# Nine due times for nine decoding steps: the weight chunks of an attention and gated-FFN kernel

## The chip, the cores and the metric

One core of a Trainium2 chip runs the whole program. The metric is the device time of one execution in microseconds (us), the median of the timed runs. Engines: TensorE (PE in the rows, its weight loads PEld), VectorE (DVE), ScalarE (ACT), GpSimd (POOL), and SyncE (SP), which here only issues DMAs.

## The reference

Attention with rotary position embedding over 8 batches × 8 heads (576 positions, 64 wide), its output taken as the input of a gated feed-forward block:

```python
q_rot, k_rot = rotate(q), rotate(k)
scores = q_rot @ k_rot.T / sqrt(64); scores -= max(scores)
attn = exp(scores) / (sum(exp(scores)) + 1e-9)
x = (attn @ v) -> [8, 576, 512]
gate_pre = sum over k of conv_w[k] * x shifted by 4 - k      # causal, 5 taps
out = (sigmoid(gate_pre) * (x @ w_val)) @ w_out
```

The weights `w_val`, `w_out` (512×512) and `conv_w` are float64 (their scale factors make them so), the rest float32. The chip has no float64, so the kernel takes the weights as pairs of 32-bit words and decodes them into two float32r parts, high and low.

## The kernel before

Two heads make a pair; 32 pairs, four to a batch. For each pair the scores come in five groups (`s0` to `s4`, `s_mm`, L253) into PSUM; VectorE takes the row maxima (`max0` to `max8`, `s_max`, L259), ScalarE the exponentials (`exp0` to `exp8`, L272). Then P is transposed. In pairs 0 to 4 (keys with the ending `e`) and in the last one this is done by TensorE (`t0` to `t7`, `th`, `tm`, `thm`, L301 to L343) with copies out of PSUM by ScalarE or VectorE (`c0` to `c7`, `ch`, `cm`, `chm`, L188 and L190); in the others VectorE transposes blocks (`turn`, L287) and DMAs move them (`move`, L292). The P·V matmuls follow (`pv4`, `pv0`, `pv1`, `pvm`, L357 to L380), and two normalisations by VectorE (`norm0`, `norm1`, L406), which also free the two accumulators. The five taps (L427, L430) make the gate. After every fourth pair the feed-forward block runs in eight pieces of each of its two stages (`f0j`, `f1j`, L456).

q and k of the next pairs are rotated meanwhile: two multiplications (`mul0`, `mul1`, L210), an addition (`add`, L214), the high part (`hi`, ScalarE, L221) and the low part (`lo`, L225), on VectorE (V) or POOL (G) by the table `PICK`.

Each weight has four chunks of 128 rows. A chunk is loaded by SP (`load_weight`, L520, 512 KB), and decoded in nine steps:

- steps 0, 1, 3, 4, 5 on VectorE (L490, L492, L495, L496, L497) and step 2 on ScalarE (L493), all 128×512, in place (`weight_step`);
- step 6, `w_high`, the high part, on ScalarE (L527);
- step 7, `w_mm`, matmuls of the residue on TensorE into a PSUM bank (L532 to L534);
- step 8, `w_low`, the low part out of that bank, on ScalarE (L188).

The chunks 0 to 3 of `w_val` are called val0 to val3 below, those of `w_out` out0 to out3. Two chunks share a buffer of the kind `big`; there are three of these, and the transposed P of each pair needs one as well. PSUM has two banks of the kind `ps_t`, shared by transposes, P·V, residues and the feed-forward block.

**The order.** Every job is put down by `at(key, base, engine, ...)`; its due time is `base + DUE[key]`. `Plan.order` works it off as a list: of all jobs whose predecessors (by tokens read and written) are in the list already, the one with the smallest due time comes next; a job that needs a buffer waits aside until one is free. Each engine runs its jobs in the order of this list. So a due time is a rank, not a time, and a job never stands before one that it depends on. Jobs of VectorE and POOL which use the port that the two share are marked `port`; a POOL job is made to wait for the last marked VectorE job ahead of it in the list (`behind`), but a VectorE job does not wait by order for POOL.

All nine steps of a chunk write the chunk's token, so each follows the one before it. Before the change they share a key:

```python
for k, (e, ns) in enumerate((v, v2, ac, v2, v, v2)):
    at(f"d{n}{c}", due + 1.6 * k, e, ns, weight_step, n, c, k, ...)
at(f"d{n}{c}", due + 9.6, *ac, w_high, n, c, ...)
at(f"d{n}{c}", due + 10.4, "PE", 1950, w_mm, n, c, ...)
at(f"d{n}{c}", due + 12.5, "A", evict(x), w_low, n, c, "ENGINE", pick="dec" + n, ...)
```

with `due = 16 + 12 * c` for `w_val` and `62 + 10 * c` for `w_out`, and the load at `due - 6`.

Of the kernel before, what the change touches and what calls it, by code (L numbers as in the profile page):

```python
# [143 lines left out]
def attn_gated_ffn(ctx: ExitStack, tc: tile.TileContext, q2, k2, v2, tab, w_val, conv_w, w_out, out, collect=None):  # L144
# [4 lines left out]
    V, A, G, T, SP = nc.vector, nc.scalar, nc.gpsimd, nc.tensor, nc.sync  # L149
# [354 lines left out]
    taps = []  # L504
# [66 lines left out]
    def evict(x):  # L571
        return {"V": (x * 1.045 + 65, False), "A": (max(x * 0.83 + 50, 280), False)}
# [6 lines left out]
    def weights(n):  # L579
        x = DM  # L580
        for c in R4:
            tok = f"big/w{n}{c // 2}#{c % 2}"
            due = (16 + 12 * c) if n == "val" else (62 + 10 * c)
            at(f"l{n}{c}", due - 6, "SP", 560, load_weight, n, c, w=tok, kb=x * 1.024)
            v, v2, ac = ("V", x * 0.522 + 90), ("V", x * 1.045 + 90), ("A", x * 0.83 + 94)
            for k, (e, ns) in enumerate((v, v2, ac, v2, v, v2)):
                at(f"d{n}{c}", due + 1.6 * k, e, ns, weight_step, n, c, k, w=tok + f" w{n}{c}#lo" * (k == 5), port=e == "V")
            at(f"d{n}{c}", due + 9.6, *ac, w_high, n, c, w=f"{tok} w{n}{c}#hi")
            at(f"d{n}{c}", due + 10.4, "PE", 1950, w_mm, n, c, r=f"{tok} w{n}{c}#hi w{n}{c}#lo", w=f"ps_t/w{n}{c}", mode="f")
            at(f"d{n}{c}", due + 12.5, "A", evict(x), w_low, n, c, "ENGINE", pick="dec" + n, r=f"ps_t/w{n}{c}", w=f"w{n}{c}#lo")  # L590
# [203 lines left out]
```

## Time and profile before

| | us |
|---|---|
| timed runs, median of 3 (lowest, highest) | 659.85 (659.34, 663.73) |
| span of the profiled execution (no other time is given for it) | 660.3 |
| TensorE busy in the span | 614.9 (93%) |
| VectorE busy | 577.5 (87%) |
| ScalarE busy | 454.5 (69%) |
| POOL busy | 398.0 (60%) |

Busy time is what the profiler saw an engine execute; matmuls overlap, so a busy TensorE is not one at its peak. In the timelines a row is a start, a duration and an instruction; a bracket tells how long the engine sat idle before it, and what ended that. In the chain of waits each row is what the next one waited for.

### The profile page before, as it was taken

How to read it: one execution, taken by the hardware profiler on the slowest of the kernel's cores; microseconds unless marked ns; L12 is line 12 of the kernel's file. 1: busy time of each engine (PE TensorE's matmuls, PEld its weight loads, DVE VectorE, ACT ScalarE, POOL GpSimd, SP SyncE). 2: the span in 40 equal slices, each digit the busy share in tenths (PEclk: the TensorE clock that was granted, in tenths of full speed). 3: DMA queues.
4: the chain of work that ended last, by engine and by line, in shares of the span. 5: the costliest groups of instructions: out<-in, count | busy, mean ns of one | idle time of the engine just before them, and what ended most of it. 6: DMA issues, size and time to landing. Idle time of an engine off the chain costs nothing.

```text
span 660.3 us, 15367 instructions
## 1 busy us (share of the span) xinstructions
PE 614.9 (93%) x5720; PEld 496.2 (75%) x5720; DVE 577.5 (87%) x829; ACT 454.5 (69%) x1120; POOL 398.0 (60%) x303
## 2 busy tenths in 40 slices
PE   2889888889999999999999999999999999999897
PEld 1666665578777887888778887888788878888696
DVE  5799988898899999999999999999999999984552
ACT  3678877677667678777777677767777777763421
POOL 3333446569577877777776868687867777730210
PEclk9999999899989999999999999999999999999999
DMA  7324432259999999899999899999998989874101
GB/s 280 119 56 142 138 129 94 88 159 253 243 258 251 248 252 267 240 260 236 263 255 261 208 274 270 252 245 265 244 256 237 249 260 258 210 179 115 38 27 64
DMA packets 51481, 134.42 MB, mean 204 GB/s; under 512 B 10928, under 2 KB 20944, under 8 KB 51408
## 3 DMA queue, kind: packets, MB, share of 16 engines
q1 hardware_dynamic: 50864, 132.86, 72.5%
q8 instruction: 45, 0.74, 0.5%
q10 hardware_dynamic: 544, 0.59, 0.3%
q14 instruction: 28, 0.23, 0.1%
HBM read 62.48 MB, written 9.59 MB: 109 GB/s over the span
## 4 chain that ended last, share of the span: by engine, by line
PE 67%; DVE 17%; DMA 5%; ACT 4%; SPq 3%; issue 2%; POOL 0%; DVEq 0%; ACTq 0%
PE ps_t L456 26%; PE ps_s L253 17%; PE ps_t L367 14%; DVE nm L259 6%; DVE big L287 3%; SPq L292 3%; DMA ik<-in_k 3%; PE ps_t L357 3%; PE ps_t L328 2%; PE ps_t L301 2%; PE ps_t L372 2%; ACT p L272 2%; DVE g L430 2%; DMA big<-big 1%; DVE big L190 1%
## 5 line engine op out<-in xcount | busy, mean ns | idle before, releaser
L272 ACT ACTIVATE p<-ps_s,nm 128x576 f32<-128x576 f32 x256 | 187.8, 739 | 80.7 <-DVE nm L259 79.4
L259 DVE TENSOR_REDUCE nm<-ps_s 128x1 f32<-128x576 f32 x288 | 202.3, 744 | 23.8 <-PE ps_s L253 23.5
L253 PE MATMUL ps_s<-k,q 64*128 64x288 f32 x1536 | 143.7, 314 | 20.1 <-ACT k L221 9.1
L253 PEld LDWEIGHTS ps_s<-k,q 64*128 64x128 f32 x1536 | 111.3, 189 | 44.3 <-ACT p L272 13.5
L287 DVE STREAM_TRANSPOSE big<-p 128x1152 f32<-128x1152 f32 x104 | 139.8, 1353 | 0.0
L430 DVE SCALAR_TENSOR_TENSOR g<-x,cw,g 128x576 f32<-128x576 f32 (+1 forms) x132 | 118.2, 895 | 2.1 <-ACT g L427 0.6
L367 PE MATMUL ps_t<-big,v 128*64 128x256 f32 (+2 forms) x1024 | 118.6, 385 | 0.0
L367 PEld LDWEIGHTS ps_t<-big,v 128*64 128x64 f32 x1024 | 70.9, 138 | 46.2 <-issue 15.1
L210 POOL TENSOR_TENSOR iq<-iq,tab 128x576 f32<-128x576 f32 (+1 forms) x59 | 84.5, 1448 | 31.2 <-DMA iq<-in_q 27.8
L214 POOL TENSOR_TENSOR ik<-ik 128x576 f32<-128x576 f32 x27 | 39.0, 1443 | 75.0 <-DVE ik L210 72.8
L456 PE MATMUL ps_t<-xh,wval_hi 128*128 128x288 f32 x256 | 78.2, 305 | 2.2 <-DVE g L461 2.0
L456 PE MATMUL ps_t<-yh,wout_hi 128*128 128x288 f32 x256 | 79.0, 309 | 1.2 <-ACT yh L465 1.1
L456 PE MATMUL ps_t<-yl,wout_hi 128*128 128x288 f32 x256 | 76.5, 299 | 0.1
L225 POOL TENSOR_TENSOR k<-ik,k 128x576 fp32r<-128x576 f32 x31 | 54.6, 1761 | 36.0 <-ACT k L221 34.0
L456 PE MATMUL ps_t<-yh,wout_lo 128*128 128x288 f32 x256 | 75.9, 297 | 0.0
L456 PE MATMUL ps_t<-xh,wval_lo 128*128 128x288 f32 x256 | 75.9, 296 | 0.0
L456 PE MATMUL ps_t<-xl,wval_hi 128*128 128x288 f32 x256 | 75.3, 294 | 0.0
L469 POOL TENSOR_TENSOR yl<-g,yh 128x288 fp32r<-128x288 f32 x56 | 46.9, 845 | 32.8 <-DVE g L430 25.3
L417 POOL TENSOR_TENSOR xl<-x,xh 128x576 fp32r<-128x576 f32 (+1 forms) x33 | 48.3, 1464 | 25.9 <-ACT xh L413 16.5
L225 POOL TENSOR_TENSOR q<-iq,q 128x576 fp32r<-128x576 f32 (+1 forms) x32 | 45.5, 1423 | 15.8 <-ACT q L221 15.8
L210 POOL TENSOR_TENSOR ik<-ik,tab 128x576 f32<-128x576 f32 (+1 forms) x32 | 45.5, 1422 | 11.7 <-DVE big L492 7.4
L456 PEld LDWEIGHTS ps_t<-xh,wval_hi 128*128 128x128 f32 x256 | 48.1, 188 | 5.7 <-DVE g L461 2.3
(89 smaller groups left out, 1065.1 us busy)
## 6 DMA issues: line engine op xcount, KB each, us to landing
big<-big SPq DMA_DIRECT2D x416, 144.0 KB
ik<-in_k SPq DMA_DIRECT2D x31, 576.0 KB
iq<-in_q SPq DMA_DIRECT2D x31, 576.0 KB
v<-in_v SPq DMA_DIRECT2D x32, 320.0 KB
rb<-rd SPq DMA_DIRECT2D x64, 144.0 KB
out_t<-oo SPq DMA_DIRECT2D x64, 144.0 KB
big<-in_w_val SPq DMA_DIRECT2D x4, 512.0 KB
big<-in_w_out SPq DMA_DIRECT2D x4, 512.0 KB
```

Source lines behind the costliest of these rows:

```text
L210: eng.tensor_tensor(out=t[:, i, a:b], in0=t[:, i, a:b], in1=tabs[:, i, a:b], op=ALU.mult)
L214: eng.tensor_tensor(out=t[:, 0], in0=t[:, 0], in1=t[:, 1], op=ALU.add)
L225: eng.tensor_tensor(out=t[:, 1], in0=state[p][n + "in"][:, 0, a:b], in1=t[:, 0].bitcast(F32), op=ALU.subtract)
L253: T.matmul(out=ps[:, half, 0:288], lhsT=st["q"][rows, x, c * 128:c * 128 + 128] if c < 4 else mixq[p % 2][:, x], rhs=st["k"][rows, y, k0:k ...
L259: V.tensor_reduce(out=st[f"nm{i}"], in_=st[f"s{i}"], axis=AX.XY, op=ALU.max, negate=True)
L272: A.activation(out=pd.rearrange("p (b x) -> p b x", b=2), in_=st[f"s{i}"], func=AF.Exp, bias=st[f"nm{i}"], scale=1.0, accum_out=sums[p % 2 ...
L287: V.transpose(out=t[:, :, cs.index(c)].rearrange("p b k i -> p k b i"), in_=st[f"p{c}"].rearrange("p h s -> p (h s)").rearrange("p (k b i) ...
L367: T.matmul(out=acc[HEAD[h], 0:n], lhsT=st["v"][:, j, h, :], rhs=st["pt"][:, :, c0:c1, 5 * place(p, 2 * c0 + h) + j].rearrange("p a c i -> ...
L417: eng.tensor_tensor(out=st["xl"][:, a:b], in0=xs[p % 2][:, 4 + a:4 + b], in1=st["xh"][:, a:b].bitcast(F32), op=ALU.subtract)
L430: V.scalar_tensor_tensor(out=g, in0=x_sb[:, a + k:b + k], scalar=w, in1=g, op0=ALU.mult, op1=ALU.add)
L456: T.matmul(out=acc[:, 0:n], lhsT=wt[w][:, kc, ds], rhs=mv, start=(kc == 0 and i == 0), stop=(kc == NCH - 1 and i == 2))
L469: eng.tensor_tensor(out=ffn[b, "l", dc, lo], in0=y, in1=ffn[b, "h", dc, lo].bitcast(F32), op=ALU.subtract)
```

## The change

The key of each step gets the number of the step, and the table `DUE` a value for each of the 72 keys instead of 8. The values of the eight loads change as well. Ten other keys go from the tables (`x0`, `x2`, `x4`, `x6`, `mv0e` to `mv3e`, `ch0`, `ch0e`, which no job uses), and the entries are in another order. All other due times, all jobs and all engines are as before.

```diff
             for k, (e, ns) in enumerate((v, v2, ac, v2, v, v2)):
-                at(f"d{n}{c}", due + 1.6 * k, e, ns, weight_step, n, c, k, w=tok + f" w{n}{c}#lo" * (k == 5), port=e == "V")
-            at(f"d{n}{c}", due + 9.6, *ac, w_high, n, c, w=f"{tok} w{n}{c}#hi")
-            at(f"d{n}{c}", due + 10.4, "PE", 1950, w_mm, n, c, r=f"{tok} w{n}{c}#hi w{n}{c}#lo", w=f"ps_t/w{n}{c}", mode="f")
-            at(f"d{n}{c}", due + 12.5, "A", evict(x), w_low, n, c, "ENGINE", pick="dec" + n, r=f"ps_t/w{n}{c}", w=f"w{n}{c}#lo")
+                at(f"d{n}{c}_{k}", due + 1.6 * k, e, ns, weight_step, n, c, k, w=tok + f" w{n}{c}#lo" * (k == 5), port=e == "V")
+            at(f"d{n}{c}_6", due + 9.6, *ac, w_high, n, c, w=f"{tok} w{n}{c}#hi")
+            at(f"d{n}{c}_7", due + 10.4, "PE", 1950, w_mm, n, c, r=f"{tok} w{n}{c}#hi w{n}{c}#lo", w=f"ps_t/w{n}{c}", mode="f")
+            at(f"d{n}{c}_8", due + 12.5, "A", evict(x), w_low, n, c, "ENGINE", pick="dec" + n, r=f"ps_t/w{n}{c}", w=f"w{n}{c}#lo")
```

What the tables come to: the due time of the load, and those of the nine steps, for the values after the change as the largest so far within the chunk, since a step cannot stand before its predecessor.

| chunk | load, before → after | steps 0 to 8 before (0, 1, 2, 3, 4, 5, 6, 7, 8) | steps 0 to 8 after, largest so far |
|---|---|---|---|
| val0 | −734.8 → −2090.8 | 13.3, 14.9, 16.5, 18.1, 19.7, 21.3, 22.9, 23.7, 25.8 | −852.7, 14.9, 14.9, 20.0, 20.0, 20.0, 20.0, 20.0, 23.0 |
| val1 | −308.0 → 15.4 | 34.5, 36.1, 37.7, 39.3, 40.9, 42.5, 44.1, 44.9, 47.0 | 39.3, 39.3, 39.3, 40.8, 40.8, 40.8, 40.8, 45.2, 49.4 |
| val2 | −178.9 → −309.8 | 29.5, 31.1, 32.7, 34.3, 35.9, 37.5, 39.1, 39.9, 42.0 | 24.8, 32.1, 32.1, 34.0, 34.0, 34.0, 38.8, 40.0, 41.8 |
| val3 | −115.4 → −137.7 | 47.7, 49.3, 50.9, 52.5, 54.1, 55.7, 57.3, 58.1, 60.2 | 49.7, 49.7, 55.6, 57.4, 57.4, 57.4, 57.4, 58.6, 60.2 |
| out0 | 89.9 → 25.5 | 103.1, 104.7, 106.3, 107.9, 109.5, 111.1, 112.7, 113.5, 115.6 | 85.7, 85.7, 87.6, 111.2, 111.2, 111.2, 111.2, 116.3, 116.3 |
| out1 | 27.9 → 55.5 | 66.2, 67.8, 69.4, 71.0, 72.6, 74.2, 75.8, 76.6, 78.7 | 67.4, 71.6, 73.0, 76.1, 76.1, 76.1, 76.1, 77.8, 80.9 |
| out2 | 33.4 → 44.6 | 84.6, 86.2, 87.8, 89.4, 91.0, 92.6, 94.2, 95.0, 97.1 | 71.2, 71.2, 78.2, 90.5, 90.5, 90.5, 116.8, 123.6, 123.6 |
| out3 | 77.0 → 47.7 | 108.5, 110.1, 111.7, 113.3, 114.9, 116.5, 118.1, 118.9, 121.0 | 89.2, 89.2, 89.2, 113.3, 121.3, 125.3, 125.3, 129.4, 129.4 |

## Rows read from the trace of the kernel before

**Rows 1.** Windows: stretch in us; length, busy time (x instructions) per engine; clock, DMA.

```profile
core 0: us, PE busy (x) PEld busy (x) DVE busy (x) ACT busy (x) POOL busy (x), PEclk, DMA share, GB/s
107.31:128.63 21.32, 17.82 (x141) 11.38 (x142) 18.69 (x27) 15.25 (x35) 12.13 (x9) 0.92 0.24 86
```

**Rows 2.** Waits of TensorE, 44.8 to 128.7 us.

```profile
engine line waited for: us in total, times, longest us
...
PE ps_t L301 <- DVE big L190: 2.2, 3, 1.1
PE ps_t L328 <- DVE big L190: 1.7, 1, 1.7
```

**Rows 3.** The chain that ended last, 0 to 13 us: start, us, what.

```profile
0.74 4.20 DMA ik<-in_k
...
6.41 0.47 DVE ik L214
...
9.02 0.60 ACT tab L206
```

**Rows 4.** Windows of the start, columns as in rows 1.

```profile
2.00:4.25 2.25, 0.00 (x0) 0.00 (x0) 0.14 (x1) 1.13 (x3) 0.00 (x0) 1.00 0.88 264
2.00:7.15 5.15, 0.00 (x0) 0.00 (x0) 1.34 (x4) 1.69 (x3) 1.00 (x2) 1.00 1.01 330
```

**Rows 5.** The decoding steps' lines: ns minimum/median/maximum, first and last start, shapes.

```profile
L490 DVE TENSOR_SCALAR big<-big x8: 414/422/1628, 13.2 to 117.0; 128x512 int32<-128x512 int32 x8
...
L492 DVE SCALAR_TENSOR_TENSOR big<-big x8: 675/692/693, 14.6 to 120.7; 128x512 int32<-128x512 int32 x8
...
L495 DVE SCALAR_TENSOR_TENSOR big<-big x8: 681/684/1844, 17.9 to 126.3; 128x512 f32<-128x512 f32 x8
...
L496 DVE TENSOR_SCALAR big<-big x8: 415/696/1621, 19.8 to 130.9; 128x512 int32<-128x512 int32 x8
...
L497 DVE SCALAR_TENSOR_TENSOR wout_lo<-big x4: 652/682/784, 80.8 to 132.6; 128x512 fp32r<-128x512 uint32 x4
```

**Rows 6.** Timeline of POOL: start, us, line, operation, out<-in.

```profile
85.36 1.41 POOL L225 TENSOR_TENSOR k<-ik,k 128x576 fp32r<-128x576 f32 x1 [6.77 <-ACT k L221]
...
97.00 2.97 POOL L210 TENSOR_TENSOR iq<-iq,tab 128x576 f32<-128x576 f32 x2 [3.81 <-DMA iq<-in_q]
...
114.62 3.69 POOL L210 TENSOR_TENSOR iq<-iq,tab 128x576 f32<-128x576 f32 x2 [0.69 <-POOL k L225]
118.39 1.47 POOL L214 TENSOR_TENSOR iq<-iq 128x576 f32<-128x576 f32 x1
```

**Rows 7.** Timeline of VectorE.

```profile
83.82 0.75 DVE L214 TENSOR_TENSOR ik<-ik 128x576 f32<-128x576 f32 x1
...
86.36 0.49 DVE L406 TENSOR_TENSOR x<-ps_t,rb 128x320 f32<-128x320 f32 x1 [1.45 <-PE ps_t L380]
...
96.36 0.68 DVE L495 SCALAR_TENSOR_TENSOR big<-big 128x512 f32<-128x512 f32 x1
97.08 1.62 DVE L496 TENSOR_SCALAR big<-big 128x512 int32<-128x512 int32 x1
...
116.97 1.63 DVE L490 TENSOR_SCALAR big<-big 128x512 int32<-128x512 int32 x1
118.52 1.62 DVE L496 TENSOR_SCALAR big<-big 128x512 int32<-128x512 int32 x1
```

**Rows 8.** Timeline of TensorE.

```profile
102.26 0.66 PE L357 MATMUL ps_t<-big,v 64*64 64x256 f32 x8
102.86 3.67 PE L367 MATMUL ps_t<-big,v 128*64 128x256 f32 x32
...
109.90 1.02 PE L534 MATMUL ps_t<-big,ident 128*128 128x512 f32 x2
...
121.38 1.86 PE L357 MATMUL ps_t<-big,v 64*64 64x256 f32 x8
...
123.17 4.68 PE L367 MATMUL ps_t<-big,v 128*64 128x256 f32 x32
```

**Rows 9.** Windows around TensorE's slow stretch, columns as in rows 1.

```profile
119.00:120.00 1.00, 0.06 (x1) 0.00 (x0) 1.00 (x1) 0.59 (x1) 0.86 (x1) 1.00 0.13 51
122.00:123.00 1.00, 0.97 (x6) 0.29 (x4) 1.00 (x2) 0.43 (x2) 0.00 (x0) 0.50 0.00 0
```

More of the change, by code (lines that the diff above doesn't have):

```diff
@@ L35 @@
-PICK = {'c0': 'A', 'c0e': 'A', 'c1': 'V', 'c1e': 'V', 'c2': 'A', 'c2e': 'A', 'c3': 'V', 'c3e': 'A', 'c4': 'A', 'c4e': 'V', 'c5': 'V', 'c5e': 'A', 'c6': 'A', 'c6e': 'V', 'c7': 'V', 'c7e': 'A', 'ch0': 'A', 'ch0e': 'V', 'ch1': 'V', 'ch1e': 'A', 'chm': 'A', 'chme': 'A', 'cm': 'A', 'cme': 'A', 'kadd': 'G', 'kadd_0': 'V', 'kadd_1': 'V', 'kadde': 'V', 'kfront': 'A', 'kfronte': 'A', 'klo': 'G', 'klo_0': 'V', 'klo_1': 'V', 'kloe': 'G', 'kmul0': 'G', 'kmul0_0': 'V', 'kmul0_1': 'V', 'kmul0e': 'V', 'kmul1': 'V', 'kmul1_0': 'G', 'kmul1_1': 'V', 'kmul1e': 'G', 'od0': 'A', 'od0l': 'A', 'od1': 'A', 'od1l': 'V', 'od2': 'A', 'od2l': 'V', 'od3': 'A', 'od3l': 'A', 'qadd': 'G', 'qadd_0': 'V', 'qadd_1': 'V', 'qadde': 'V', 'qlo': 'G', 'qlo_0': 'V', 'qlo_1': 'G', 'qloe': 'G', 'qmixed': 'A', 'qmixede': 'A', 'qmul0': 'G', 'qmul0_0': 'G', 'qmul0_1': 'V', 'qmul0e': 'V', 'qmul1': 'G', 'qmul1_0': 'V', 'qmul1_1': 'V', 'qmul1e': 'G', 'xlo': 'G', 'xloe': 'G', 'xlol0': 'G', 'xlol1': 'G', 'ylo': 'G', 'ylol': 'V', 'ch3': 'A', 'ch3e': 'V', 'decout': 'A', 'decval': 'A', 'odma': 'SP', 'odmal': 'SP', 'loadk': 'SP', 'loadk_0': 'SP', 'loadk_1': 'SP', 'loadke': 'SP', 'loadq': 'SP', 'loadq_0': 'SP', 'loadq_1': 'SP', 'loadqe': 'SP', 'loadv': 'SP', 'loadve': 'SP', 'mv0': 'SP', 'mv1': 'SP', 'mv2': 'SP', 'mv3': 'SP', 'rr': 'SP', 'rre': 'SP', 'rw': 'SP', 'rwe': 'SP'}
@@ new lines @@
+PICK = {'loadk_0': 'SP', 'kmul0_0': 'V', 'kmul1_0': 'G', 'kadd_0': 'V', 'klo_0': 'V', 'loadk_1': 'SP', 'kmul0_1': 'V', 'kmul1_1': 'V', 'kadd_1': 'V', 'klo_1': 'V', 'loadq_0': 'SP', 'qmul0_0': 'G', 'qmul1_0': 'V', 'qadd_0': 'V', 'qlo_0': 'V', 'loadq_1': 'SP', 'qmul0_1': 'V', 'qmul1_1': 'V', 'qadd_1': 'V', 'qlo_1': 'G', 'kfronte': 'A', 'qmixede': 'A', 'loadve': 'SP', 'c0e': 'A', 'c1e': 'V', 'c2e': 'A', 'c3e': 'A', 'c4e': 'V', 'c5e': 'A', 'c6e': 'V', 'c7e': 'A', 'ch1e': 'A', 'ch3e': 'V', 'cme': 'A', 'chme': 'A', 'rwe': 'SP', 'rre': 'SP', 'xloe': 'G', 'decval': 'A', 'decout': 'A', 'loadke': 'SP', 'kmul0e': 'V', 'kmul1e': 'G', 'kadde': 'V', 'kloe': 'G', 'loadqe': 'SP', 'qmul0e': 'V', 'qmul1e': 'G', 'qadde': 'V', 'qloe': 'G', 'ylo': 'G', 'od0': 'A', 'odma': 'SP', 'od1': 'A', 'od2': 'A', 'od3': 'A', 'loadk': 'SP', 'kmul0': 'G', 'kmul1': 'V', 'kadd': 'G', 'klo': 'G', 'loadq': 'SP', 'qmul0': 'G', 'qmul1': 'G', 'qadd': 'G', 'qlo': 'G', 'kfront': 'A', 'qmixed': 'A', 'loadv': 'SP', 'mv0': 'SP', 'mv1': 'SP', 'mv2': 'SP', 'mv3': 'SP', 'cm': 'A', 'chm': 'A', 'rw': 'SP', 'rr': 'SP', 'xlo': 'G', 'c0': 'A', 'c1': 'V', 'c2': 'A', 'c3': 'V', 'c4': 'A', 'c5': 'V', 'c6': 'A', 'c7': 'V', 'ch1': 'V', 'ch3': 'A', 'xlol0': 'G', 'xlol1': 'G', 'ylol': 'V', 'od0l': 'A', 'odmal': 'SP', 'od1l': 'V', 'od2l': 'V', 'od3l': 'A'}
```

2 lines of the change are left out of this document (1 added, 1 removed).

## The prediction

> **What bounds the kernel now.** I read the windows first. While the weights are decoded, VectorE is at least as full as TensorE: from normalisation to normalisation of pair 4 it has 18.69 us of 21.32, TensorE 17.82 [rows 1]. Then the waits of TensorE: in pairs 1 to 4 the PSUM copies on VectorE are late for it by 2.2 us in three waits and once by 1.7 us [rows 2]. Last the timelines, pair by pair. Each pair has a stretch in which VectorE hardly rests (from the end of the second normalisation of the pair before to the PSUM copy `c4`), and one in which TensorE runs the P·V matmuls and VectorE ends up idle, 1.45 us before the second normalisation at 86.36 [rows 7]. A decoding step in the first stretch is paid for; in the second it is free, until that idle time is used up. So the question of each moved step is in which stretch it lands, and what POOL does there.
>
> **How the new places follow.** The planner starts, among the jobs that are ready, the one with the smallest due time, and the steps of a chunk follow each other; so a step's place is set by the largest due time so far in its chunk (the table in the section on the change). I place each against the due times of its neighbours, worked out from `at` and the table: `norm0` of pairs 0 to 4 at 39.3, 57.8, 76.3, 94.8, 113.3; `kadd` ahead of it at 57.1 (in pair 1) and 75.6 (pair 2); `max0` and `max1` of pair 4 at 88.7 and 91.2. Nothing is added or removed: eight instructions of each step before and after. The plain lengths of the VectorE steps 0, 1, 3, 4, 5 are 0.42, 0.69, 0.68, 0.42, 0.68 us [rows 5]. Steps 0, 3 and 4 have maxima of 1.63, 1.84 and 1.62 us there: such an instruction began while POOL had one running and ended just after it. The pair 97.08 with 1.62 us on VectorE and 97.00 on POOL (2.97 us for two) shows it [rows 6, 7].
>
> **The start, +1.6 us.** The load of chunk 0 of w_val gets due −2090.8 and is issued ahead of the second half of k; its step 0 gets −852.7, ahead of `kadd_0` (−537.0). VectorE works in order, so `kadd_0` now waits for the weight. `kadd_0` is the VectorE piece at 6.41 us on the chain that leads through POOL and the table's scaling to the first scores [rows 3]; nothing covers it. Bytes: two table halves, two q/k pieces, the taps and the weight are 288+288+288+256+20+512 KB = 1.69 MB, and up to 7.15 us the DMA engines moved 330 GB/s × 5.15 us = 1.70 MB [rows 4]. The first k half had its bytes (0.59 MB = 264 GB/s × 2.25 us) at 4.25 us and released VectorE at 4.94 [rows 3, 4], 0.7 us later. So the weight is seen at 7.15 to 7.85, and with 0.42 us for the step `kadd_0` begins at 7.6 to 8.3 instead of 6.41: 1.2 to 1.9, I take 1.6. Below it can hardly be less than 1.1; if the two loads issued behind it (288+320 KB, at the same 330 GB/s 1.9 us) share the engines fully, it is up to 3.0. The other early loads change places among equal sizes, and the out loads come earlier than before; SP issues those behind waits for chunks that are decoded long before, so I cost them at nothing.
>
> **Pair 0, 0.** Before `c4` stood steps 0, 1, 3 of chunk 2 (one stretched to 1.84) and step 0 of chunk 1, 3.4 us; now stand steps 1, 3, 4, 5 of chunk 2, 2.5 us plain, beside the same POOL multiplication, which can stretch one by up to 1.4. Between −0.9 and +0.5, I take 0.
>
> **Pair 1, +0.3.** Steps 3 to 5 of chunk 1 go to the front, steps 3 and 4 of chunk 3 leave for the P·V stretch. That takes a stretched step 4 away from before `c4`, and the copy's wait there (one of the three of 2.2 us, longest 1.1 [rows 2]) shrinks; I take −0.5. But steps 3, 4, 5 of chunk 3 (57.4) now stand between `kadd` (57.1) and `norm0` (57.8). What POOL does there is seen in the same place of pair 2: `kadd` ends at 84.57, ACT rounds, and POOL runs its subtraction from 85.36 for 1.41 us [rows 6, 7]. See pair 2 for the price: +0.8. Bounds of the sum: −1.0 (no POOL conflict) to +1.1.
>
> **Pair 2, +0.8.** The steps before `c4` are step 0 of out1, 0 and 1 of out2, 1 of out1, as long as those of before (2.2 us). Steps 3, 4, 5 of out1 (76.1) move between `kadd` and `norm0`, where before only step 5 stood, ahead of the taps. Without that one `kadd` ends 0.6 earlier, at 83.95, and POOL begins at 84.75; step 3 runs to 84.6, step 4 to 84.9, step 5 waits for POOL's end at 86.15 and ends at 86.8; `norm0` (some 0.4 ahead of the next instruction, as the second one, 0.49 long [rows 7]) lets the second normalisation begin at 87.2 instead of 86.36: +0.8. Without the conflict step 5 ends at 85.5 and the idle 1.45 us hides it all: 0. At most 1.2, if POOL's next instruction goes first.
>
> **Pair 3, +2.7.** This is the term that decides. Between `max0` and `max1` of pair 4 stood steps 3 and 4 of out2, from 96.36 to 98.70, one stretched [rows 7]; now stand steps 0 and 1 of out3 (89.2) and 3, 4, 5 of out2 (90.5). Plain, that is 0.42+0.69+0.68+0.42+0.68 less the overlaps of some 0.06 each, 2.6 us, against 2.3: +0.3. POOL has two multiplications there from 97.00 in 2.97 us, released by a DMA that shifts along [rows 6], and then the addition `qadd`, as long as one of them: 4.4 us. Steps 3, 4, 5 then meet them. The nearest rows are those against three POOL instructions from 114.62 to 119.86: the steps at 116.97 and 118.52, one right behind the other, took 1.63 and 1.62 [rows 6, 7], two waits of 1.2 in a row. I take two: 0.3+2.4 = 2.7. Ends: +0.3 with none, +3.9 with three.
> The Trainium skill, "SBUF — State Buffer", section "Who interferes with whom", says that a VectorE instruction with two SBUF inputs, or in a two-port mode, and a POOL instruction exclude each other for the whole instruction, by order of issue. The stretched rows agree; by it all three steps would wait (+3.9), without it none (+0.3).
>
> **Pair 4, −1.9.** Before `c4` stood five steps, of 0.42, 0.69, 0.69, 1.63 and 1.62 us; now none: steps 0 and 1 of out0 are in pair 3, steps 3 to 5 after `max0` of pair 5, under P·V. TensorE's wait of 1.7 us goes [rows 2], and some 0.2 of smaller ones: −1.9. Next is TensorE's own chain, and the fuller P·V stretch (7.1 us of VectorE work against some 6.9 of TensorE). If the durations of all five steps came back it would be −5.0; if that stretch is late, −0.5. The clock: after 119 to 120 us, with TensorE busy 0.06, the granted clock was 0.50, the level of 1.2 GHz, at 122 [rows 9], and the two P·V groups took 1.86 and 4.68 us instead of 0.66 and 3.67 [rows 8]: 2.2 us. With a longer gap now in pair 3 (1.1+2.7), I let this loss move there: net 0.
>
> **After pair 4, 0.** Chunk 2 of out is multiplied later (its last two matmuls took 1.02 us [rows 8], with the two ahead an estimated 1.5), in a stretch where TensorE is full; up to +1.5, taken as 0 since pair 4 gives up the same time. What is late or early at 150 us stays so to the end, as all that follows hangs on the pairs before it.
>
> **Sum.** 1.6 + 0 + 0.3 + 0.8 + 2.7 − 1.9 + 0 = +3.5 us on the profiled span of 660.3, 663.8. The median of the timed runs (659.85) lies 0.45 below that span, so 663.3. Adding the terms' bounds by squares gives about ±3: 660.3 to 666.4.
>
> **Rivals.** (a) *POOL's instructions fall past the steps.* If its q load lands later than the five steps of pair 3, and `norm0` of pairs 1 and 2 is not held, the terms are 1.6, 0, −0.5, 0, +0.3, −1.9, and the clock does not fall at all (−2.2): −2.7, 657.1; with pair 4 at −5.0, the start at 1.1 and pair 0 at −0.9 it is 652.7. For it: VectorE gets out of its fullest stretch in pair 4. Against: in pair 3 POOL has 4.4 us of work and the five steps plain only 2.6.
> (b) *Slower: all three steps of pair 3 wait and the clock falls in pair 3 and once more in pair 4.* The place is between `max0` and `max1` of pair 4; +3.9 instead of +2.7 and one more fall of the clock, 2.2: 666.7. It decides from the point where TensorE's gap before `t3` of pair 3 exceeds the 1.7 us after which the clock fell before. For it: the gap would be 1.1+3.9 = 5.0. Against: the nearest rows have two waits and no third.
> (c) *The change does less than it says:* steps with equal due times run as one block, as before, and early losses vanish behind waits for loads later: 659.9.
>
> **How the numbers follow.** The sum 0.46, (a) 0.28, (b) 0.20, (c) 0.06. A measurement of this kernel can tell about 1% from no change, 653.25 to 666.45. Half of (a), where pair 4, pair 0 and the start come near those bounds, is faster by more: 0.14. All of (b) and the uppermost 0.03 of the sum are slower by more: 0.23. The rest, 0.63, lies within. The range of 8 in 10 takes in most of (a), and (b) with 1.8 of lateness elsewhere (the start at 3.0, a conflict in pair 0): 655.5 to 668.5; the likeliest case alone is 660.3 to 666.4.
>
> **What would show it.** Start: `kadd_0` at 7.6 to 8.3 us with VectorE idle before step 0, and the first scores 1.6 later. Pairs 1 and 2: a step 5 of 1.5 us or more just before `norm0`, and no idle time before the second normalisation. Pair 3: stretched steps between `max0` and `max1`, and the copy wait of TensorE up from 1.1 to about 3.8 us. Pair 4: no copy wait. I am wrong if `kadd_0` stays at 6.4, if these steps show plain lengths, or if the time is gained or lost after 150 us.

## The result, and the profile after

| | before | after |
|---|---|---|
| timed runs, median of 12 each (lowest to highest), us | 663.41 (659.34 to 666.55) | 672.00 (666.64 to 674.73) |
| ratio after/before, 95% interval | | 1.0132 (1.0105 to 1.0158) |
| span of the profiled execution, us | 660.3 | 667.3 |
| mean granted clock of TensorE | 0.995 | 0.989 |

The change made the kernel slower by 8.6 us in the medians and by 7.0 in the spans of the two profiles, where +3.5 and 663.3 had been forecast; 672.0 lies above the range of 655.5 to 668.5. Part of the distance is in the base: the three runs of before that the forecast stood on have the median 659.85, twelve runs 663.41, 3.6 more. The rest, 5.1 us, is the change itself. The profiled execution of after (669.10) is the third shortest of its twelve, so the terms read from it below add up to 7.0 and not to 8.6.

All ratios, here and in the experiments, are worked out from the single runs in the faster of the two states that executions fall into, and they differ from the quotient of the two medians by up to 0.25%.

I cut the span at the second normalisation of each pair. Windows of after, from that of pair 0 to that of pair 4 (columns as in [rows 1]):

```profile
46.10:69.60 23.50, 19.95 (x167) 13.45 (x167) 21.84 (x34) 17.29 (x40) 7.43 (x5) 1.00 0.37 123
69.60:90.33 20.73, 18.00 (x163) 12.65 (x163) 19.77 (x32) 16.00 (x38) 8.49 (x6) 1.00 0.40 139
90.33:117.38 27.05, 20.00 (x164) 13.87 (x165) 21.50 (x31) 16.49 (x39) 12.81 (x9) 0.87 0.25 84
117.38:137.98 20.60, 18.52 (x147) 13.46 (x146) 14.31 (x24) 13.58 (x32) 7.81 (x6) 0.83 0.20 67
```

In before these normalisations began at 44.80, 66.30, 86.36, 107.31 and 128.63, so pairs 1 to 4 took 21.50, 20.06, 20.95 and 21.32 us. Pair 3 is the stretch to look at: 6.1 us longer, at a mean granted clock of 0.87. Pair 4 answers to [rows 1]: VectorE lost 4.4 us of work there (18.69 to 14.31), as planned, but the pair is only 0.7 us shorter, at a mean granted clock of 0.83.

Waits of TensorE, 46 to 138 us of after:

```profile
PE ps_t L301 <- DVE big L190: 5.0, 3, 4.4
...
PE ps_t L301 <- DVE x L406: 1.6, 2, 1.0
```

Against [rows 2]: the wait of 1.7 us behind L328 is gone, one of 4.4 us has come, and so have two for a normalisation (L406), which do not stand among those of before. Where the 4.4 us come from is seen with the timelines of VectorE and POOL beside each other. VectorE, at the end of pair 2 and in pair 3:

```profile
88.23 1.78 DVE L497 SCALAR_TENSOR_TENSOR wout_lo<-big 128x512 fp32r<-128x512 uint32 x1
89.93 0.81 DVE L406 TENSOR_TENSOR x<-ps_t,rb 128x256 f32<-128x256 f32 x2
...
100.15 0.42 DVE L490 TENSOR_SCALAR big<-big 128x512 int32<-128x512 int32 x1
100.60 0.69 DVE L492 SCALAR_TENSOR_TENSOR big<-big 128x512 int32<-128x512 int32 x1
101.21 1.92 DVE L495 SCALAR_TENSOR_TENSOR big<-big 128x512 f32<-128x512 f32 x1
103.16 1.51 DVE L496 TENSOR_SCALAR big<-big 128x512 int32<-128x512 int32 x1
104.71 1.77 DVE L497 SCALAR_TENSOR_TENSOR wout_lo<-big 128x512 fp32r<-128x512 uint32 x1
106.40 1.41 DVE L259 TENSOR_REDUCE nm<-ps_s 128x1 f32<-128x576 f32 x2
107.73 0.68 DVE L190 COPY big<-ps_t 128x512 f32<-128x512 f32 x1
```

POOL in the same stretches:

```profile
87.91 1.55 POOL L225 TENSOR_TENSOR k<-ik,k 128x576 fp32r<-128x576 f32 x1 [5.89 <-ACT k L221]
...
100.94 3.44 POOL L210 TENSOR_TENSOR iq<-iq,tab 128x576 f32<-128x576 f32 x2 [3.82 <-DMA iq<-in_q]
104.47 1.46 POOL L214 TENSOR_TENSOR iq<-iq 128x576 f32<-128x576 f32 x1
```

Steps 3 to 5 of out2 (from 101.21) and three POOL instructions alternate. POOL's began at 100.94, 102.54 and 104.47, each just ahead of a step (101.21, 103.16, 104.71), and the three steps took 5.20 us for what takes 0.68 + 0.42 + 0.68 = 1.78 [rows 5]. The maxima and the copy at 107.73 queue behind them, and TensorE waits for that copy:

```profile
108.46 1.11 PE L301 MATMUL ps_t<-ident,p 128*128 128x128 f32 x4 [4.44 <-DVE big L190]
109.51 1.81 PE L253 MATMUL ps_s<-k,q 64*128 64x288 f32 x12
111.24 1.13 PE L357 MATMUL ps_t<-big,v 64*64 64x256 f32 x8
112.30 4.30 PE L367 MATMUL ps_t<-big,v 128*64 128x256 f32 x32
...
120.78 1.80 PE L253 MATMUL ps_s<-k,q 64*128 64x288 f32 x11 [0.90 <-ACT p L272]
```

In before the same copy was late by 1.07 us:

```profile
100.68 0.66 PE L301 MATMUL ps_t<-ident,p 128*128 128x128 f32 x4 [1.07 <-DVE big L190]
```

The two P·V groups took 0.66 and 3.67 us at full clock in pair 3 of before [rows 8]; here they took 1.13 and 4.30. Windows of 1 us tell why (columns as in [rows 1], the granted clock is the third number from the end):

```profile
105.00:106.00 1.00, 0.00 (x0) 0.00 (x0) 1.00 (x1) 0.00 (x0) 0.93 (x1) 1.00 0.35 111
106.00:107.00 1.00, 0.00 (x0) 0.00 (x0) 1.00 (x2) 0.00 (x0) 0.00 (x0) 0.89 0.00 0
107.00:108.00 1.00, 0.00 (x0) 0.00 (x0) 1.00 (x3) 0.82 (x3) 0.00 (x0) 0.50 0.00 0
...
118.00:119.00 1.00, 0.46 (x3) 0.23 (x4) 1.00 (x2) 1.00 (x3) 0.35 (x1) 1.00 0.02 9
...
120.00:121.00 1.00, 0.22 (x2) 0.22 (x4) 1.00 (x2) 1.00 (x4) 0.06 (x1) 0.72 0.00 0
121.00:122.00 1.00, 1.00 (x10) 1.00 (x11) 0.09 (x1) 1.00 (x3) 0.00 (x0) 0.50 0.00 0
```

During and after the stop of TensorE the granted clock is 0.50 (1.2 GHz) from 107 to 113, and after pauses of 0.54 and 0.90 us in pair 4 once more from 121 to 127. Up to this point before had one such stretch, in pair 4, 122 to 125 [rows 9].

The start, from the chain that ended last (start, us, what), answers to [rows 3]:

```profile
3.00 5.39 DMA big<-in_w_val
...
8.42 0.43 DVE big L490
8.84 0.38 DVE ik L214
```

The weight is now on the chain; `kadd_0` begins at 8.8 instead of 6.41, and the first full group of scores at 14.64 instead of 12.30.

### The profile page after: what moved, and what is told of

Same layout as the page of the kernel before. It is cut to its first block, busy times and chain, and to the rows that moved or that the text cites. A ratio compares the mean times of both kernels' runs of the same rounds, so it can differ in the third digit from the quotient of the medians.

```text
span 667.3 us, 15366 instructions
## 1 busy us (share of the span) xinstructions
PE 614.6 (92%) x5720; PEld 496.4 (74%) x5720; DVE 582.6 (87%) x829; ACT 453.5 (68%) x1120; POOL 397.2 (60%) x303
## 4 chain that ended last, share of the span: by engine, by line
PE 69%; DVE 20%; ACT 4%; DMA 2%; issue 2%; SPq 1%; POOL 0%; DVEq 0%; ACTq 0%
PE ps_t L456 28%; PE ps_s L253 18%; PE ps_t L367 13%; DVE nm L259 6%; DVE big L287 4%; DVE g L430 3%; PE ps_t L357 2%; PE ps_t L328 2%; PE ps_t L301 2%; ACT p L272 2%; PE ps_t L372 2%; DMA big<-big 1%; DVE big L190 1%; DVE ik L210 1%; SPq L292 1%
## 5 line engine op out<-in xcount | busy, mean ns | idle before, releaser
L272 ACT ACTIVATE p<-ps_s,nm 128x576 f32<-128x576 f32 x256 | 187.6, 738 | 80.9 <-DVE nm L259 79.4
L259 DVE TENSOR_REDUCE nm<-ps_s 128x1 f32<-128x576 f32 x288 | 202.0, 743 | 21.4 <-PE ps_s L253 20.8
L253 PE MATMUL ps_s<-k,q 64*128 64x288 f32 x1536 | 146.0, 316 | 23.9 <-ACT k L221 11.4
L253 PEld LDWEIGHTS ps_s<-k,q 64*128 64x128 f32 x1536 | 112.7, 190 | 48.9 <-ACT p L272 15.5
L430 DVE SCALAR_TENSOR_TENSOR g<-x,cw,g 128x576 f32<-128x576 f32 (+1 forms) x132 | 119.9, 908 | 2.1 <-ACT g L427 0.6
L367 PEld LDWEIGHTS ps_t<-big,v 128*64 128x64 f32 x1024 | 70.7, 137 | 46.0 <-issue 14.9
L225 POOL TENSOR_TENSOR k<-ik,k 128x576 fp32r<-128x576 f32 x31 | 56.1, 1810 | 30.4 <-ACT k L221 28.8
L417 POOL TENSOR_TENSOR xl<-x,xh 128x576 fp32r<-128x576 f32 (+1 forms) x33 | 48.8, 1479 | 30.9 <-ACT xh L413 19.8
L225 POOL TENSOR_TENSOR q<-iq,q 128x576 fp32r<-128x576 f32 (+1 forms) x32 | 45.0, 1406 | 18.6 <-ACT q L221 18.6
L456 PEld LDWEIGHTS ps_t<-yh,wout_hi 128*128 128x128 f32 x256 | 48.2, 188 | 4.6 <-DVE x L406 2.7
```

The costliest lines, as they stand in the source:

```text
L225: eng.tensor_tensor(out=t[:, 1], in0=state[p][n + "in"][:, 0, a:b], in1=t[:, 0].bitcast(F32), op=ALU.subtract)
L253: T.matmul(out=ps[:, half, 0:288], lhsT=st["q"][rows, x, c * 128:c * 128 + 128] if c < 4 else mixq[p % 2][:, x], rhs=st["k"][rows, y, k0:k ...
L259: V.tensor_reduce(out=st[f"nm{i}"], in_=st[f"s{i}"], axis=AX.XY, op=ALU.max, negate=True)
L272: A.activation(out=pd.rearrange("p (b x) -> p b x", b=2), in_=st[f"s{i}"], func=AF.Exp, bias=st[f"nm{i}"], scale=1.0, accum_out=sums[p % 2 ...
L367: T.matmul(out=acc[HEAD[h], 0:n], lhsT=st["v"][:, j, h, :], rhs=st["pt"][:, :, c0:c1, 5 * place(p, 2 * c0 + h) + j].rearrange("p a c i -> ...
L417: eng.tensor_tensor(out=st["xl"][:, a:b], in0=xs[p % 2][:, 4 + a:4 + b], in1=st["xh"][:, a:b].bitcast(F32), op=ALU.subtract)
```

## The experiments

Each run's ratio is against runs of before on the same chip. Most differences are small against their intervals, so two ratios are called different below only where the intervals allow it. In the diffs only the changed entries of `DUE` stand; those of the runs e... start from the kernel after, those of the runs b... from the kernel before.

| run | median, us | of before, us | ratio (95%) |
|---|---|---|---|
| e1_start | 667.28 | 661.96 | 1.0074 (1.0039 to 1.0108) |
| e2_pair3 | 663.89 | 661.96 | 1.0021 (0.9988 to 1.0054) |
| e3_pool | 665.70 | 661.96 | 1.0070 (1.0029 to 1.0112) |
| e4_cover | 673.73 | 661.96 | 1.0164 (1.0100 to 1.0228) |
| e5_front | 669.26 | 662.70 | 1.0101 (1.0068 to 1.0135) |
| e6_three | 660.44 | 662.70 | 0.9966 (0.9942 to 0.9990) |
| e7_four | 661.42 | 662.70 | 0.9981 (0.9954 to 1.0009) |
| b1_pair4 | 661.44 | 662.70 | 0.9991 (0.9965 to 1.0018) |
| b3_start | 664.79 | 662.59 | 1.0023 (0.9996 to 1.0050) |
| b4_out | 668.58 | 662.59 | 1.0084 (1.0050 to 1.0118) |
| e8_five | 662.72 | 662.59 | 1.0007 (0.9974 to 1.0040) |
| b5_pair4b | 659.51 | 662.89 | 0.9924 (0.9895 to 0.9952) |

**Step 0 of val0 back behind the start (e1_start).**

```diff
-'dval0_0': -868.72716
+'dval0_0': -2.73
```

> The changed kernel with step 0 of val0 alone back at its old due time (13.3); its load stays early. In-order theory: the addition of the first k half no longer waits for the weight's load, starts at about 6.5 us instead of 8.76, everything behind it is some 2.3 us earlier, and the time falls by about 2.3 us (ratio to before about 1.010 instead of 1.013). Rival (the loads' new order delays k and q themselves, the step only fills an idle engine): the addition stays late, above 8 us, and the time stays.

Measured: `kadd_0` at 6.51, the first scores at 12.40, as before, though the weight is still loaded early. So it is VectorE's wait for the weight that costs, not the order of the loads. The ratio falls by 0.6% (1.0132 to 1.0074), where the 2.3 us seen at the start are 0.35%; the two intervals together allow some 0.1 to 1.0%.

**Steps 3 to 5 of out2 behind max3 of pair 4 (e2_pair3).**

```diff
-'dout2_3': 3.68154, 'dout2_4': -2796.61344, 'dout2_5': -9.79982
+'dout2_3': 5.8, 'dout2_4': 4.2, 'dout2_5': 2.6
```

> The changed kernel with steps 3, 4, 5 of out2 moved from between the maxima 0 and 1 of pair 4 to behind maximum 3, under the P.V matmuls of pair 3. Theory (these three wait for POOL and hold the PSUM copy, and the gap lets the clock fall): TensorE's wait of 4.4 us for the copy falls under 1 us, no window with a granted clock of 0.50 between 104 and 128 us or at most one short one, second normalisation of pair 3 to 4 some 5 us earlier, time lower by 4 to 7 us. Rival (pair 3 is late for other reasons, or the steps cost as much under the P.V matmuls): less than 2 us.

Measured: no copy on VectorE holds TensorE in pair 3 any more, the clock stays at 1.00 there, pair 3 takes some 20.6 us instead of 27.05, and the ratio falls from 1.0132 to 1.0021. Step 4 still meets POOL (1.52 us), but in the P·V stretch, where nobody waits for it. This place holds most of the loss. In pair 4 the clock fell all the same (0.50 from 115 to 121), and that pair took 20.5 us, as in after: that fall does not need the stop in pair 3.

**POOL's instructions behind the steps (e3_pool).** The steps stay where they are; the first multiplication of q for pair 5 gets a later due time.

```diff
-                for key, d, fn, arg, rd, wr in (("mul0", 0, rope_mul, (0,), th + f" seq{n}", x0),
+                lag = 5.9 * (p == 5 and n == "q")
+                for key, d, fn, arg, rd, wr in (("mul0", lag, rope_mul, (0,), th + f" seq{n}", x0),
```

> The changed kernel with the due time of POOL's first q multiplication of pair 5 raised by 5.9, so that POOL's three instructions wait for step 5 of out2; VectorE's order stays. Port theory: steps 3, 4, 5 of out2 take their plain 0.68, 0.43, 0.68 us instead of 1.92, 1.51, 1.77, the copy wait falls from 4.4 to about 1 us, the falls of the clock go, time lower by 4 to 6 us. Rival (it is the amount of VectorE work ahead of the copy, the stretched durations only show a wait that would appear elsewhere): copy wait stays above 3 us, time within 1 us.

VectorE in pair 3 of this run:

```profile
99.91 1.92 DVE L495 SCALAR_TENSOR_TENSOR big<-big 128x512 f32<-128x512 f32 x1
101.87 0.43 DVE L496 TENSOR_SCALAR big<-big 128x512 int32<-128x512 int32 x1
102.33 0.69 DVE L497 SCALAR_TENSOR_TENSOR wout_lo<-big 128x512 fp32r<-128x512 uint32 x1
```

POOL ran one multiplication at 99.57 and the next only at 103.11, behind the steps. Step 3 still takes 1.92, steps 4 and 5 have their plain length, and TensorE's wait falls from 4.4 to 2.3 us. The same steps in the same place: their length is POOL's doing. The ratio falls to 1.0070. The expectation came true in part only: one meeting of three was left, the wait did not go down to 1 us, and the clock still fell twice (0.50 from 107 to 110 and from 117 to 120).

**Steps 3 to 5 of val3 and out1 ahead of the taps (e4_cover).**

```diff
-'dval3_3': 0.60129, 'dval3_4': -1530.56111, 'dval3_5': -3417.84554
+'dval3_3': -0.9, 'dval3_4': -2.5, 'dval3_5': -4.1
-'dout1_3': -0.69507, 'dout1_4': -2248.19801, 'dout1_5': -19.47288
+'dout1_3': -2.6, 'dout1_4': -4.2, 'dout1_5': -5.8
```

> The changed kernel with steps 3, 4, 5 of val3 and out1 ahead of the taps instead of between the addition and the first normalisation (same stretch, same work, before POOL's subtraction). Port theory: both steps 5 take 0.68 us instead of 1.78; the normalisations of pairs 1 and 2 are no longer late, TensorE's waits for them (1.6 us in two) go, time lower by 1.5 to 2.5 us. Rival (the stretch is simply too full by now, whatever the order): TensorE's waits stay, time within 0.7 us.

A miss: 1.0164, from four runs, no better than after. Steps 3 to 5 are plain in both pairs, but two other waits came, as VectorE's timeline shows:

```profile
65.88 0.69 DVE L495 SCALAR_TENSOR_TENSOR big<-big 128x512 f32<-128x512 f32 x1 [1.71 <-ACT big L493]
...
81.44 2.53 DVE L492 SCALAR_TENSOR_TENSOR big<-big 128x512 int32<-128x512 int32 x2
```

In pair 1 VectorE, ahead of its old place, waited 1.71 us for step 2 on ScalarE, which kept its due time; in pair 2 other steps met POOL instead, and the clock fell at 88.

**Step 5 of val1 out of the front of pair 1 (e5_front).**

```diff
-'dval1_5': -3036.18273
+'dval1_5': 5.7
```

> The kernel after, with step 5 of val1 moved behind max5 and c1 of pair 1, so that it no longer meets POOL's instruction xl (VectorE 1.79 us at 47.78, POOL 1.65 at 47.38). Theory (this step's stretch of 1.1 us is paid in pair 1): the first scores' maxima and the copy after them come 1.8 us earlier, TensorE's idle 1.12 before its matmul at 51.16 goes, pair 1 lasts some 22.4 us instead of 23.5, and the time falls by about 1 us, to 671. Rival (pair 1's length comes from the late second normalisation at its end alone): pair 1 still ends with VectorE's stretched step at 67 us and a normalisation no more than 0.3 us earlier; 672.

The step takes 0.68 instead of 1.79 us and pair 1 some 22.3 instead of 23.5, as the theory had it. The ratio falls by 0.3%, which the two intervals cannot tell from nothing. Its profile is 4.0 us shorter than that of after, more than this step explains: pair 0, which the edit does not touch, ended 1.7 us earlier, and in pair 4 the clock did not fall (see the last two sections).

**The three together (e6_three).** The edits of e1_start, e2_pair3 and e5_front.

> The kernel after, with three changes at once: step 0 of val0 back to its due time of before (13.27), steps 3 to 5 of out2 behind max3 of pair 4, step 5 of val1 behind c1 of pair 1. Theory (the losses sit in these places and add up; alone the first two gave 4.7 and 8.1 us): what is left of the loss is the late second normalisations in pairs 1 and 2, about 2 us together, against 0.7 to 1.7 gained in pair 4, so 660 to 663, as fast as before within 0.4%. Rival (the places share one loss, since a later stage waits for whatever is latest): no better than with the steps of out2 alone, 663.5 to 665.

The theory holds: 1.0132 becomes 0.9966, by 1.7%, where the three alone gave 0.6, 1.1 and 0.3%. With three places mended the change is slightly faster than the kernel before, though its profile still has three falls of the clock (from 39, 83 and 114 us).

**And the steps ahead of the taps, with their step 2 early (e7_four).** The edits of e6_three and of e4_cover, and

```diff
-'dval3_2': 0.34987, 'dout1_2': -2.20735
+'dval3_2': -4.26, 'dout1_2': -5.83
```

> As the run with three changes, and also steps 3 to 5 of val3 and of out1 ahead of the taps (due 55.9 and 74.2), this time with their step 2 on ScalarE at its old due times 50.94 and 69.37, so that VectorE finds it done. Theory: the stretched step 5 before norm0 in pairs 1 and 2 takes its plain 0.7 us, VectorE is idle before the second normalisation again, and 1 to 2 us go: 659 to 661.5. Rival (the three steps meet POOL's multiplications of the next k and q wherever they stand in the P·V stretch): equal to the run with three changes within 1 us, with a stretched step in a new place.

Pairs 1 and 2 took 21.4 and 20.4 us, as expected, but the total did not improve (0.9981 and 0.9966 overlap). With the steps ahead of it `kadd` of pair 2 ended 19.5 us after that pair's start (87.87 - 68.39) instead of 17.5 in after, and POOL's instructions behind it met the next pair's VectorE work: in pair 3 a multiplication took 1.73 instead of 0.75 us, the two steps of out3 still there 1.55 and 1.79, TensorE waited 1.97 us for the exponentials, the clock fell at 97, and the pair took 23.7 us. The rival had the time right, and that stretched steps would turn up in a new place.

**Pair 4 alone relieved, from the kernel before (b1_pair4).** Each step has its key, with the chunk's old value except these; the first two lines are the old values of the two chunks.

```diff
-'dout0': 41.08
-'dout3': 16.46
+'dout0_4': 42.85, 'dout0_5': 41.25
+'dout3_0': 19.5, 'dout3_1': 17.9, 'dout3_3': 16.56
```

> The kernel before (all due times of loads and steps as there), with only the relief of pair 4 taken over: step 4 of out0 and step 0 of out3, the two stretched ones at 118.52 and 116.97, stand behind the copy c4 of pair 4 (due 111.25 and 111.5; with them step 5 of out0 and step 1 of out3), and step 3 of out3 behind the normalisation. Theory (those two are what made TensorE wait 1.7 us and lose its clock at 120): the wait of 1.7 us goes and the clock stays at 1.00, -1.7 and -2.2: 658 to 659, at best 2 us more from matmuls that meet no stop. Rival (ScalarE and the scores hold TensorE at the same place, and the clock falls all the same, as it did in the run with the steps of out2 moved): -0.5 to 0, 661.5 to 662.

In pair 4 there was no wait of 1.7 us and no fall of the clock, and the pair took some 18.5 us instead of 21.3. Yet the time is a miss: 661.44 where 658 to 659 was expected, 0.9991 and not clear of 1. From the second normalisation of pair 4 to that of pair 5 (161.65, in before 162.16) it took 36.1 us instead of 33.5: 2.6 of the 2.8 us were given back. VectorE at the front of pair 5:

```profile
125.86 1.40 DVE L495 SCALAR_TENSOR_TENSOR big<-big 128x512 f32<-128x512 f32 x1
...
128.52 1.67 DVE L496 TENSOR_SCALAR big<-big 128x512 int32<-128x512 int32 x1
```

Steps 3 and 4 of out3, beside POOL again, ahead of the first maxima and of the first transpose of pair 5.

**The start alone, added to before (b3_start).** The loads of after, and `'dval0_0': -868.72716`.

> The kernel before, with only two things taken over: the due times of the eight loads, and that of step 0 of val0 (-852.7). Theory (the wait of kadd_0 for the weight, 2.0 to 2.4 us, is on the path and nothing later hides it; the loads' order alone costs nothing): first scores at 14.3 to 14.6 instead of 12.3, and 664 to 665 us. Rival (the wait is made up for in pair 0, where that step is then missing ahead of w_mm): 662.7 to 663.5.

Scores 2 us late, 2.5 late at the second normalisation of pair 0; 1.0023 (0.9996 to 1.0050), 1.5 us. It fits the theory, but the interval shuts out neither the rival nor no change at all.

**The w_out chunks alone, added to before (b4_out).** The dues of all four out chunks and the loads of after.

> The kernel before for w_val (steps at their old due times), the kernel after for all four chunks of w_out, and the loads of after. Theory (pair 3's three waits behind POOL make the loss by themselves, whatever went before): TensorE stands for some 4.4 us before the copies in pair 3, its clock is 0.50 behind that, and the time is 666 to 669 us. Rival (pair 3 hurts only because the pairs before it are late against the q load, or the loss of the clock is chance): under 664.

1.0084, 5.6 us. TensorE in pair 3:

```profile
104.36 0.90 PE L301 MATMUL ps_t<-ident,p 128*128 128x128 f32 x3 [4.43 <-DVE big L190]
```

The same wait as in after, to 0.01 us, and the same two falls of the clock, with the steps of w_val as they were before. So the places of w_val's steps have no part in it.

**Four more steps moved (e8_five).** The edits of e6_three and

```diff
-'dval2_5': -3080.02883, 'dval3_2': 0.34987, 'dval3_3': 0.60129, 'dval3_4': -1530.56111, 'dval3_5': -3417.84554
+'dval2_5': -12.1, 'dval3_2': -4.26, 'dval3_3': -0.9, 'dval3_4': -2.5, 'dval3_5': -4.1
-'dout3_0': -2.76343, 'dout3_1': -3300.28172
+'dout3_0': 11.1, 'dout3_1': 11.1
```

> As the run with three changes, and four steps more are put where VectorE has time: step 5 of val2 behind c4 of pair 0 (it took 1.85 us ahead of it), steps 3 to 5 of val3 ahead of the taps with step 2 at its old due time (out1 stays as in after), and steps 0 and 1 of out3 from pair 3 to the first third of pair 4 (due 103.1, 104.7), where VectorE waits for TensorE anyway. Theory: the copy wait in pair 0 falls from 1.7 to under 1 us, pair 1 to 21.4, no stretched step is left ahead of a copy, the clock stays at 1.00, and pairs 0 to 4 end 3 to 5 us earlier than with three changes: 656 to 659. Rival (what is gained before 130 us is held back by the next limit in pair 5, as in the run that relieved pair 4 alone): 659.5 to 661.

A miss: 1.0007. Up to the second normalisation of pair 3 all went as expected (104.7 us, before 107.31). Then ScalarE, which takes its jobs in order, waited 1.10 us for step 1 of out3 with a copy that TensorE needs queued behind that wait:

```profile
113.79 1.74 PE L253 MATMUL ps_s<-k,q 64*128 64x288 f32 x11 [1.30 <-ACT k L188]
```

and the clock was 0.50 from 114 to 120. A step's due time moves not only the step but the place of the next one on another engine.

**Pair 4 relieved, and out3 where after has it (b5_pair4b).** As b1_pair4, with steps 0 and 1 of out3 in the P·V stretch of pair 3, its steps from 3 on and all loads as after, and the rest as before.

```diff
-'dout0': 41.08
-'dout3': 16.46
+'dout0_4': 42.85, 'dout0_5': 41.25
+'dout3_0': 0.6, 'dout3_1': -1.0
+'dout3_3': 16.48392, 'dout3_4': 22.93758, 'dout3_5': 25.25351
```

> The kernel before for w_val, out1, out2 and the first four steps of out0; loads as after; pair 4 relieved as in the earlier run (steps 4 and 5 of out0 behind c4, due 111.25), but steps 0 and 1 of out3 stand in the P·V stretch of pair 3 (due 92.6), and its steps 3, 4 and 5 where after has them (113.3, 121.3, 125.3). Theory (the earlier run lost its 2.8 us in pair 5, since steps 3 and 4 of out3 stood at that pair's front beside POOL, 1.40 and 1.67 us long): pair 4 lasts 18.5 us, from there to the second normalisation of pair 5 it is 33.3 to 34 instead of 36.1, and the time is 659.5 to 660.5. Rival (pair 5 cannot start earlier whatever VectorE does, held by the exponentials or the loads): the normalisation of pair 5 stays near 161.6 us, 661.5 to 662.5.

0.9924 (0.9895 to 0.9952), from six runs: faster than both kernels, by 0.8% against before in the ratio and by 3.4 us in the medians. VectorE in pairs 4 and 5:

```profile
120.67 0.42 DVE L496 TENSOR_SCALAR big<-big 128x512 int32<-128x512 int32 x1
...
124.84 0.68 DVE L495 SCALAR_TENSOR_TENSOR big<-big 128x512 f32<-128x512 f32 x1
...
159.83 0.49 DVE L406 TENSOR_TENSOR x<-ps_t,rb 128x320 f32<-128x320 f32 x1 [1.67 <-PE ps_t L380]
```

No step is stretched in pair 4, and pair 5 ends at 159.83, though pair 0 was 0.5 us later than in before; from pair 4 to pair 5 it took 34.0 us, as expected. So pair 5 could start earlier, and b1_pair4 most likely lost its gain to the places of out3's steps. This run has the loads of after as well, which b1_pair4 has not, and no run tells the two apart. It is the only profile without any fall of the clock from 20 to 200 us.

## Why the prediction was wrong, point by point

Two steps of the sum failed, both in its sizes and not in the idea that VectorE's steps wait for POOL: "I take two" in pair 3, where three waits came, and "I let this loss move there: net 0", where the clock fell twice. A step left uncounted in pair 1 comes third. The measured terms are differences of the second normalisations of the two profiles; where both normalisations stand in one row (x2), the second begins some 0.4 us after the first. In the forecast the 2.2 us of clock loss stand in the pairs between which they were to move.

| step | forecast | measured |
|---|---|---|
| start (first scores) | +1.6 | +2.3 |
| pair 0 | 0 | -1.0 |
| pair 1 | +0.3 | +2.0 |
| pair 2 | +0.8 | +0.7 |
| pair 3 | +4.9 (2.7, and 2.2 of clock loss) | +6.1 |
| pair 4 | -4.1 (-1.9, and the 2.2 gone) | -0.7 |
| after pair 4 | 0 | -2.4 |
| sum | +3.5 | +7.0 |

- **The start: right in mechanism, too small.** The weight released VectorE at 8.4 us, not at 7.15 to 7.85: the two loads issued behind it shared the DMA engines, which I had kept for the upper bound (3.0). From 2 to 8.39 us they moved 332 GB/s × 6.39 us = 2.12 MB, where the weight and all ahead of it are 1.69.
- **Pair 0: a number that is luck.** After, e2_pair3, e3_pool, e4_cover and e5_front have one order up to here, and yet their second normalisations came at 46.10, 46.96, 44.80, 46.98 and 44.40. Two things differ. Step 5 of val2, ahead of `c4`, races with a multiplication of POOL: in after, e2_pair3 and e4_cover it began 0.03 to 0.30 us behind it (35.64 and 35.52 in after) and took 1.85, 1.94 and 1.79 us; in e3_pool and e5_front it began 0.22 and 0.06 us ahead of it and took 0.69, and POOL took 1.73 and 1.90 instead of 1.42. The copy wait is 1.71 to 1.85 us in the first three and 0.61 in the other two (0.92 in before). And the first matmuls are slow in all kernels, and became fast at different times: the two of L534 took 1.02 us in after (at 26.2), e3_pool and e5_front, and 1.91 in e2_pair3, e4_cover and before (at 26.9), though the granted clock reads 1.00 for all.
- **Pair 1: a step left uncounted.** "Steps 3 to 5 of chunk 1 go to the front" had no price; step 5 met a subtraction of POOL there (L417) and took 1.79 us, and without that e5_front has a pair 1 that is 1.2 us shorter. The conflict ahead of `norm0` was foreseen, and so was that of **pair 2**: step 5 took 1.78 us, and the pair was longer by 0.7 us, forecast 0.8.
- **Pair 3: the step that failed is "I take two".** I had counted waits after a pattern in the rows [rows 6, 7] and not by what POOL had to do here. The pattern itself had three steps, and I left out the first:

```profile
116.36 0.69 DVE L495 SCALAR_TENSOR_TENSOR big<-big 128x512 f32<-128x512 f32 x1
```

  It had begun ahead of POOL's second multiplication (116.49), so that meeting was POOL's to wait for, and two were left for VectorE. In pair 3 of after POOL was ahead in all three meetings. From the first of the five steps to the end of the last it took 6.33 us (100.15 to 106.48) instead of 2.34 for the two of before (96.36 to 98.70): 4.0 more, which is the bound for three waits (+3.9). TensorE's wait for the copy grew by 3.4 (4.44 - 1.07). e2_pair3 and e3_pool show the cause from both sides, and b4_out that w_val's steps have no part in it. The Trainium skill, "SBUF — State Buffer", section "Who interferes with whom", says that of two such instructions the one issued first holds the shared ports to its end and the other blocks; this trace agrees (1.92, 1.51 and 1.77 us behind POOL), and so do the two orders in pair 0.
- **The clock: "I let this loss move there: net 0" failed too.** It fell in pair 3 and again in pair 4. In pair 3 the groups at 108.46, 109.51, 111.24 and 112.30 took 8.35 us; such groups at full clock take 0.66, 1.20, 0.66 and 3.67, which makes 2.2 us. In pair 4, e5_front has the same steps and no fall and took 18.6 us, where after took 20.6: the relief of the pair was worth 2.7 us (21.3 - 18.6) and not 4.1, and the new fall took 2.0 of it. Part of the 4.1 was a misreading: the first P·V group took 1.25 us in pair 4 of after at full clock too (at 131.61), so the old fall had cost about 1.6 us and not 2.2.
- **Why a second fall.** The prediction gave no reason for one, and (b) hung it on a gap above 1.7 us in pair 3, which its own likeliest case (1.1 + 2.7) had as well. The runs point elsewhere. In before the residue matmuls of out2 (109.32 to 110.92) stand between a transpose and the scores in pair 4. Where they are moved behind, TensorE instead pauses 0.90 us there for the exponentials: in after, all the runs e... and b4_out, and not in before, b1_pair4, b3_start and b5_pair4b, which keep them. In seven of these ten profiles the clock fell at that pause, in e2_pair3 and e6_three without any long stop in pair 3 (not in e5_front, e7_four and e8_five). The prediction has that move under "After pair 4", taken as 0. No run moves step 7 of out2 alone, so this is argued and not shown.
- **Rival (b)** forecast +6.9 (666.7); the spans differ by 7.0, the medians by 8.6. It had the three waits and the two falls right, but the closeness in the spans is partly luck: its terms for pairs 1 and 4 were off by 1.7 and 1.2, pair 0 is luck, and 2.4 came back after pair 4, where before had a slow stretch from 186 to 190 us and after had none.
- **The base.** Had I taken the profiled execution (span 660.3, and some 1.7 to 2.6 us around it, as in all the runs here where both are known) and not the median of three, the forecast would have been 2 to 3 us higher.

## What to carry to other kernels

Where two engines exclude each other instruction by instruction, count the instructions of both that meet, ask for each meeting who begins first, and price one wait for each that your engine loses: here a block of three steps lost three times. It costs only where something that another engine needs is queued behind. Where the lead is some tenths of a microsecond, as in pair 0, one order has two times, and a single profile shows one of them. Moving one step of a chain over several engines moves the next step's queue as well: look at each engine's order again, not only at the one that was full, and at what work leaves a place where it covered a wait. And a stop of TensorE can have a second price, the slow clock behind it, so a place that ends a stop may be worth more than its microseconds. From the same table of 72 values mainly those for pair 4, with most others left as they were, gave 0.8%.

## What was not expected of the hardware

The clock does not answer alike to the same stop. In pair 0 of e1_start and of e7_four TensorE waited the same 1.71 us for the same copy:

```profile
38.09 0.66 PE L301 MATMUL ps_t<-ident,p 128*128 128x128 f32 x4 [1.71 <-DVE big L190]
```

```profile
38.87 0.85 PE L301 MATMUL ps_t<-ident,p 128*128 128x128 f32 x4 [1.71 <-DVE big L190]
```

The first line is of e1_start, where the clock stayed at 1.00; the second of e7_four, where it was 0.50 from 40 to 42 us. For 8 us ahead of this stop TensorE's rows are the same in both, to 0.01 us, only 0.78 us later in e7_four. Of the six profiles with such a stop there (1.71 to 1.85 us: after, e1_start, e2_pair3, e4_cover, e6_three, e7_four) the clock fell in two. In pair 4, after and e5_front have the same pauses of 0.54 and 0.90 us behind the same steps; after fell to 0.50 at 121, e5_front stayed at 1.00. One profiled execution thus tells that a stop can cost the clock, not that it will. That this and the race in pair 0 make the spread of the times (666.64 to 674.73 for after) is likely, but was not shown.
